# Two pairs of products of 64 stationary columns each made one product of 128, in a gated delta-rule layer followed by a GELU MLP

## Chip, cores, metric

One core of a Trainium2 chip. The metric is the device time of one execution in microseconds; several executions of each kernel on the same chip are compared. An execution counts as slow when its time is over 1.5% above the fastest of the same kernel; otherwise it is fast, and only fast ones are compared; a kernel that ran only once has no known state. The inputs are fp32, except for the two weight matrices of the MLP: these arrive as 64-bit words (a piece of 128 x 512 is 512 KB in the DMA list), and VectorE and ScalarE decode them to fp32 in the first part of the kernel. All products are fp32.

## The reference

```python
# deltanet: per batch and head, a 48 x 48 state, over 768 steps
k_n = k / (norm(k) + 1e-6)
for t in range(S):                       # B, H, S, D = 4, 8, 768, 48
    y[t]  = q[t] @ state
    v_old = state.T @ k_n[t]
    state = state + beta[t] * outer(k_n[t], v[t] - v_old)
# then, on y laid out as (3072, 384):
h = x @ w_in                             # 384 -> 2048
g = 0.5 * h * (1 + erf(h / sqrt(2)))
out = g @ w_out                          # 2048 -> 384
```

The kernel works in 12 chunks of 64 steps. A chunk is two units (`a` = 0, 1), each with 2 batches x 8 heads. With K, Q, V the chunk's rows and S the state, a unit needs K S and Q S, a triangular solve that gives U, then P^T U (P the masked products of K with Q) for its output and K^T U for the next state. These are small: contraction 48 or 64, 48 moving columns. (A product loads one operand, `lhsT`, into TensorE's array and streams the other, `rhs`, through it; they are called stationary and moving, and the trace lists the load as LDWEIGHTS on "PEld" and the streaming as MATMUL on "PE".) Between them TensorE does the MLP of the previous chunk: psH (first layer) and psO (second), with 128 x 128 stationary tiles. Other names in the timelines: psU is the solve, psG the products of K with K and Q, psJ joins the halves of the elimination that prepares the solve, and psT, psX and psB are transposes.

## The kernel before

A product of 64 x 64 uses a quarter of the 128 x 128 array, and the loops go round the four quarters. The part that a product uses is called its tile, rows x columns; a tile change below is a switch between products of different tile shape. In `QUADS` the first number is the half of the rows, the second that of the columns (in `next_state` the other way round). Every product is fp32 and shows as two instructions in the trace (two MATMUL, two LDWEIGHTS), so 16 products are 32 instructions.

```python
QUADS = [(0, 0), (1, 1), (0, 1), (1, 0)]
SIDES = [(0, 0), (1, 0), (0, 1), (1, 1)]

def state_product(u, x, psum):                      # x = 0: K S,  x = 1: Q S
    for j in range(NP):
        for r, p in QUADS:
            rows = slice(r * C, r * C + D)
            nc.tensor.matmul(psum(p, j, r), lhsT=u.KQt[rows, j, p, x, :],     # 64 columns
                             rhs=St[rows, u.a, p, j, :], start=True, stop=True)

def against_state(u):
    # ... (chunk 0 cut)
    state_product(u, 0, lambda p, j, r: psK[HALF[p], r, j, :])
    nc.vector.tensor_tensor(heads(u.W), psK, heads(u.V), op=ALU.subtract)
    nc.vector.tensor_tensor(u.W, u.W, gm..., op=ALU.mult)

def query(u):
    state_product(u, 1, lambda p, j, r: psQ[HALF[p ^ (j % 2)], j // 2, j % 2, r, :])
    for r in range(2):
        nc.scalar.copy(heads(u.y)[:, r], psQ[...])

def read(u):                                         # P^T U
    for k in range(NP // 2):
        for r in range(2):
            for p, s in SIDES:
                h = 4 * k + 2 * s + r
                nc.tensor.matmul(psY[HALF[p ^ s], p, h, :], lhsT=u.P[HALF[p], h, :],
                                 rhs=u.U[HALF[p], h, :], start=True, stop=True)
    # ... four additions of 64 x 192: x = psY + y

def next_state(u):                                   # K^T U
    for j in range(NP):
        for r, p in QUADS:
            nc.tensor.matmul(psS[HALF[r], p, j, :], lhsT=u.Kp[HALF[p], 2 * j + r, :],
                             rhs=u.U[HALF[p], 2 * j + r, :], start=True, stop=True)
    nc.vector.tensor_tensor(St[:, u.a], St[:, u.a], psS, op=ALU.add)

def state_steps(c):
    us = [tiles[c, a] for a in range(NA)]
    steps = [(1.0, fn, u) for fn in (against_state, query, solve, next_state, read) for u in us]
    return steps + [(0.5, turn, u) for u in us]
```

## Time and profile before

| | before |
|---|---|
| time, median | 755.5 us (754.5 to 755.7, 4 runs) |
| span of the profiled run | 753.3 us |
| TensorE busy, 170 us to the end | 577.2 of 583.3 us |
| VectorE busy, 60 to 170 us | 104.4 of 110 us |
| granted TensorE clock (share of full speed), whole span | 0.99 |

The table splits the span because two engines take turns in setting it: VectorE up to about 170 us, TensorE after that. The prediction shows the lines that say so. "Burst" below means one run of small products between full-size ones, and its price is the time from its start to the next burst's start, less what the full-size products between them stream for.

### The profile page before, as it was taken

How to read it: one execution, taken by the hardware profiler on the slowest of the kernel's cores; microseconds unless marked ns; L12 is line 12 of the kernel's file. 1: busy time of each engine (PE TensorE's matmuls, PEld its weight loads, DVE VectorE, ACT ScalarE, POOL GpSimd, SP SyncE). 2: the span in 40 equal slices, each digit the busy share in tenths (PEclk: the TensorE clock that was granted, in tenths of full speed). 3: DMA queues.
4: the chain of work that ended last, by engine and by line, in shares of the span. 5: the costliest groups of instructions: out<-in, count | busy, mean ns of one | idle time of the engine just before them, and what ended most of it. 6: DMA issues, size and time to landing. Idle time of an engine off the chain costs nothing.

```text
span 753.3 us, 19282 instructions
## 1 busy us (share of the span) xinstructions
PE 704.0 (93%) x8532; PEld 508.5 (68%) x8532; DVE 376.4 (50%) x855; ACT 249.4 (33%) x602; POOL 84.7 (11%) x91
## 2 busy tenths in 40 slices
PE   6549786899999999999999999999999999999997
PEld 5347553576687687687587687687687687586774
DVE  6988999996329722329822329822329821210100
ACT  3335633422553134352134352133352132122120
POOL 5051001203110002110012010012020010000000
PEclk9999999998999999999999999999999999999999
DMA  9807544400311101211101211001001000000000
GB/s 150 199 25 206 131 125 129 103 1 19 60 33 23 32 13 32 44 32 23 34 13 32 44 32 23 12 12 23 12 12 23 12 12 2 11 12 1 22 1 21
DMA packets 84515, 32.90 MB, mean 44 GB/s; under 512 B 77328, under 2 KB 80400, under 8 KB 84432
## 3 DMA queue, kind: packets, MB, share of 16 engines
q1 hardware_dynamic: 78384, 26.36, 16.0%
q10 hardware_dynamic: 5952, 5.12, 3.0%
q8 instruction: 67, 1.10, 0.6%
q0 software_dynamic: 96, 0.20, 0.1%
q14 instruction: 16, 0.13, 0.1%
HBM read 26.94 MB, written 4.72 MB: 42 GB/s over the span
## 4 chain that ended last, share of the span: by engine, by line
PE 77%; DVE 19%; issue 2%; DMA 1%; POOL 1%; ACT 0%; ACTq 0%; POOLq 0%; DVEq 0%
PE psO L544 30%; PE psH L535 30%; DVE tmp L359 3%; DVE Nu L361 3%; PE psT L283 2%; PE psG L293 2%; DVE w_e L204 2%; PE psU L470 2%; PE psJ L404 2%; PE psS L509 2%; PE psQ L447 2%; PE psK L447 2%; PE psJ L407 2%; PE psY L493 1%; DVE w_e L194 1%
## 5 line engine op out<-in xcount | busy, mean ns | idle before, releaser
L544 PE MATMUL psO<-w_out_sb,g 128*128 128x384 f32 x768 | 272.9, 500 | 10.2 <-DVE w_out_sb L205 10.2
L535 PE MATMUL psH<-xT,w_in_sb 128*128 128x256 f32 x1152 | 274.9, 388 | 3.4 <-DVE w_in_sb L205 3.0
L535 PEld LDWEIGHTS psH<-xT,w_in_sb 128*128 128x128 f32 x1152 | 213.1, 191 | 37.4 <-DVE w_in_sb L205 3.5
L544 PEld LDWEIGHTS psO<-w_out_sb,g 128*128 128x128 f32 x768 | 140.4, 192 | 97.2 <-DVE w_out_sb L205 15.6
L538 ACT ACTIVATE g<-psH 128x256 f32<-128x256 f32 x192 | 73.5, 383 | 177.4 <-PE psH L535 177.1
L361 DVE TENSOR_TENSOR Nu<-Nu,tmp 128x30 f32<-128x30 f32 (+9 forms) x180 | 61.9, 344 | 6.2
L359 DVE TENSOR_TENSOR tmp<-Nu 128x30 f32<-128x30 f32 (+9 forms) x180 | 61.8, 343 | 5.6
L253 POOL TENSOR_TENSOR n<-n,half 128x16 f32<-128x16 f32 x10 | 29.5, 2947 | 222.6 <-DVE n L242 222.6
L501 DVE TENSOR_TENSOR x<-psY,y 64x192 f32<-64x192 f32 x88 | 31.0, 353 | 42.3 <-PE psY L493 41.4
L307 DVE TENSOR_TENSOR P<-psG,mask 128x512 f32<-128x512 f32 x20 | 13.7, 690 | 72.8 <-ACT G L301 72.7
L512 DVE TENSOR_TENSOR St<-St,psS 128x384 f32<-128x384 f32 x22 | 12.2, 553 | 75.4 <-PE psS L509 75.0
L459 DVE TENSOR_TENSOR W<-psK,V 128x384 f32<-128x384 f32 x22 | 12.2, 555 | 73.6 <-PE psK L447 56.8
L475 ACT COPY U<-psU 64x192 f32<-64x192 f32 x92 | 28.8, 313 | 46.8 <-PE psU L470 46.0
L548 ACT COPY o_sb<-psO 128x384 f32<-128x384 f32 x24 | 11.5, 479 | 89.3 <-PE psO L544 89.3
L293 PE MATMUL psG<-KQt 48*64 48x128 f32 (+1 forms) x896 | 30.4, 286 | 3.9 <-ACT KQt L284 2.7
L522 ACT COPY xT<-psX 128x384 f32<-128x384 f32 x24 | 11.4, 477 | 68.0 <-PE psX L521 67.9
L293 PEld LDWEIGHTS psG<-KQt 48*64 48x64 f32 x896 | 24.9, 157 | 10.6 <-issue 4.8
L284 ACT COPY KQt<-psT 128x512 f32<-128x512 f32 x48 | 26.5, 589 | 9.1 <-PE psT L283 8.6
L383 POOL MEMSET Zf<- 32x512 f32 x23 | 12.2, 529 | 147.5 <-DVE Zf L374 145.5
L404 PE MATMUL psJ<-XM,G 32*32 32x32 f32 x768 | 15.5, 198 | 13.6 <-DVE XM L370 13.6
L415 DVE TENSOR_TENSOR XM<-psJ,gm 32x512 f32<-32x512 f32 (+1 forms) x26 | 16.9, 649 | 20.4 <-PE psJ L404 20.1
L196 ACT ACTIVATE w_e<-w_e,lim 128x384 uint32<-128x384 uint32 (+2 forms) x31 | 19.4, 625 | 23.0 <-DVE w_e L194 22.8
(100 smaller groups left out, 584.9 us busy)
## 6 DMA issues: line engine op xcount, KB each, us to landing
Qp<-in_q_dram SPq DMA_DIRECT2D x48, 96.0 KB, 3.4
V<-in_v_dram SPq DMA_DIRECT2D x48, 96.0 KB, 2.9
w_out_sb<-in_moe_w_in_dram SPq DMA_DIRECT2D x9, 512.0 KB, 5.3
out_dram<-o_sb ACTq DMA_DIRECT2D x48, 96.0 KB, 2.2
Zf<-in_moe_w_out_dram SPq DMA_DIRECT2D x8, 384.0 KB, 3.5
w_raw<-in_moe_w_out_dram SPq DMA_DIRECT2D x8, 384.0 KB, 3.1
Kp<-in_k_dram SPq DMA_DIRECT2D x28, 96.0 KB, 3.1
w_out_sb<-in_moe_w_in_dram SPq DMA_DIRECT2D x6, 256.0 KB, 4.4
```

Source lines behind the costliest of these rows:

```text
L253: nc.gpsimd.tensor_tensor(flat, flat, half, op=ALU.pow)
L284: nc.scalar.copy(u.KQt[:, :, :, x, :], psT.rearrange("q j (p n) -> q j p n", p=2))
L293: nc.tensor.matmul(psG[HALF[p], r, j, cols], lhsT=u.KQt[rows, j, p, 0, :], rhs=u.KQt[rows, j, p].rearrange("q x n -> q (x n)")[:, cols], s ...
L359: nc.vector.tensor_tensor(tmp, nu[:, j + 1:, j:j + 1].to_broadcast([128, n, j]), nu[:, j:j + 1, 0:j].to_broadcast([128, n, j]), op=ALU.mult)
L361: nc.vector.tensor_tensor(nu[:, j + 1:, 0:j], nu[:, j + 1:, 0:j], tmp, op=ALU.add)
L404: nc.tensor.matmul(psJ[low_, 0, col], lhsT=raw[top, u, HB:C], rhs=xm[top, u, :], start=True, stop=True)
L447: nc.tensor.matmul(psum(p, j, r), lhsT=u.KQt[rows, j, p, x, :], rhs=St[rows, u.a, p, j, :], start=True, stop=True)
L475: copies[i % len(copies)](pairs(u.U[HALF[p]], s), pairs(psU[HALF[p ^ s], p], s))
L501: nc.vector.tensor_tensor(dst, src, pairs(u.y[HALF[p ^ s]], s), op=ALU.add)
L535: nc.tensor.matmul(psH, lhsT=w_in_sb[:, m, f * 128:(f + 1) * 128], rhs=xTs[c][:, m, :], start=(m == 0), stop=(m == NM - 1))
L538: nc.scalar.activation(gs[f], psH, ACT.Gelu)
L544: nc.tensor.matmul(u.psO, lhsT=gs[f][:, u.a * 128:(u.a + 1) * 128], rhs=w_out_sb[:, f, :], start=(f == 0), stop=(f == NF - 1))
```

## The change

K^T and Q^T of a unit already lie beside each other in SBUF, so one product with 128 stationary columns gives K S in the lower 64 output partitions and Q S in the upper 64. For K^T U with P^T U the same is reached by putting P next to K, for which K is loaded from DRAM a second time.

```diff
-    NKS, NQS, NKW = 6, 4, 10
+    NKS, NQS = 4, 4
+    KP = [cpool.tile([128, H, 2, C], F32, name=f"KP{i}") for i in range(4)]
 ...
+    def place(c):
+        for a in range(NA):
+            u = tiles[c, a]
+            u.KP = KP[u.n % 4 if u.n < 8 else (u.n - 4) % len(KP)]
+            u.P = u.KP[:, :, 1, :]
+            fetch_in(u.KP[:, :, 0, 0:D], k, u)
 ...                                        # against_state
+        for p in range(2):
+            for j in range(NP):
+                for r in range(2):
+                    rows = slice(r * C, r * C + D)
+                    nc.tensor.matmul(psK[:, r, p, j, :],
+                                     lhsT=u.KQt[rows, j, p].rearrange("q x n -> q (x n)"),
+                                     rhs=St[rows, u.a, p, j, :], start=True, stop=True)
+        for p in range(2):
+            nc.vector.tensor_tensor(heads(u.W[HALF[p]]), psK[HALF[0], :, p], heads(u.V[HALF[p]]),
+                                    op=ALU.subtract)
         nc.vector.tensor_tensor(u.W, u.W, gm..., op=ALU.mult)
+        u.y = wk.tile([128, H, D], F32, tag="y", name="y")
+        for p in range(2):
+            nc.scalar.copy(heads(u.y[HALF[p]]), psK[HALF[1], :, p])
 ...
+    def use(u):
+        for h in range(H):
+            for p in range(2):
+                nc.tensor.matmul(u.psY[:, p, h, :],
+                                 lhsT=u.KP[HALF[p], h].rearrange("q x n -> q (x n)"),
+                                 rhs=u.U[HALF[p], h, :], start=True, stop=True)
 ...                                        # next_state: two additions of 64 x 384 from psY
 ...                                        # read: two additions of 64 x 384 from psY
-        steps = [(1.0, fn, u) for fn in (against_state, query, solve, next_state, read) for u in us]
+        steps = [(1.0, fn, u) for fn in (against_state, solve, outputs) for u in us]
```

Cut: the loads' places in the plan, the hand-ordered first chunk, the memsets of the padding.

More of the change, by code (lines that the diff above doesn't have):

```diff
@@ L86 @@
     tiles = {}
-    K_late = []
     def fetch_in(dst, src, u, queues=(nc.sync, nc.sync)):
@@ L100 @@
             u.Qp = Qp[u.n % NQS]
-            if u.n < NKW:
-                u.Kp = Kp[u.n % NKS]
+            u.Kp = Kp[u.n % NKS]
     def load(c):
@@ L108, in load @@
             u = tiles[c, a]
-            if u.n >= NKW:
-                u.Kp = K_late[(u.n - NKW) % len(K_late)]
             fetch_in(u.Kp[:, :, 0:D], k, u)
             fetch_in(u.Qp[:, :, 0:D], q, u)
+    def place(c):
+        if c >= NC:
+            return
+        for a in range(NA):
[3 more added lines that the diff above has]
+            fetch_in(u.KP[:, :, 0, 0:D], k, u)
     def load_v(c):
@@ L135 @@
         nc.gpsimd.memset(Kp[i][:, :, D:], 0.0)
+        nc.gpsimd.memset(KP[i][:, :, 0, D:], 0.0)
     for p in range(2):
@@ L302, in products @@
         if 1 in part:
-            u.P = wk.tile([128, H, C], F32, tag="P", name="P", bufs=6)
             if u.c < 2:
@@ L440 @@
     SIDES = [(0, 0), (1, 0), (0, 1), (1, 1)]
-    def state_product(u, x, psum):
-        for j in range(NP):
-            for r, p in QUADS:
-                rows = slice(r * C, r * C + D)
-                nc.tensor.matmul(psum(p, j, r), lhsT=u.KQt[rows, j, p, x, :],
-                                 rhs=St[rows, u.a, p, j, :], start=True, stop=True)
     def against_state(u):
@@ L452, in against_state @@
         gm = gms[u.c // 2][:, u.t]
+        u.y = None
         if u.c == 0:
@@ L456, in against_state, with solve @@
             return
-        psK = dn("psK")[:, :, 0:NP * D].rearrange("q r (j d) -> q r j d", d=D)
-        state_product(u, 0, lambda p, j, r: psK[HALF[p], r, j, :])
-        nc.vector.tensor_tensor(heads(u.W), psK, heads(u.V), op=ALU.subtract)
+        psK = dn("psK")[:, :, 0:2 * NP * D].rearrange("q r (p j d) -> q r p j d", p=2, d=D)
+        for p in range(2):
[8 more added lines that the diff above has]
+                                    op=ALU.subtract)
         nc.vector.tensor_tensor(u.W, u.W, gm.unsqueeze(2).to_broadcast([128, H, D]),
                                 op=ALU.mult)
-    def solve(u, copies=(nc.scalar.copy,)):
+        u.y = wk.tile([128, H, D], F32, tag="y", name="y")
+        for p in range(2):
+            nc.scalar.copy(heads(u.y[HALF[p]]), psK[HALF[1], :, p])
+    def solve(u, copy=nc.scalar.copy):
         zf = Zf[(u.c // 2) % 2]
@@ L473, in solve, with read @@
         u.U = wk.tile([128, H, D], F32, tag="U", name="U")
-        for i, (p, s) in enumerate(SIDES):
-            copies[i % len(copies)](pairs(u.U[HALF[p]], s), pairs(psU[HALF[p ^ s], p], s))
-    def query(u):
-        u.y = None
-        if u.c == 0:
-            return
-        psQ = dn("psQ")[:, :, 0:NP * D].rearrange("q r (k s d) -> q k s r d", s=2, d=D)
-        state_product(u, 1, lambda p, j, r: psQ[HALF[p ^ (j % 2)], j // 2, j % 2, r, :])
-        u.y = wk.tile([128, H, D], F32, tag="y", name="y")
-        for r in range(2):
-            nc.scalar.copy(heads(u.y)[:, r], psQ[:, :, :, r, :].rearrange("q k s d -> q (k s) d"))
-    def read(u, copies=(nc.scalar.copy,)):
-        psY = dn("psY")[:, :, 0:DM].rearrange("q p (h d) -> q p h d", d=D)
-        for k in range(NP // 2):
-            for r in range(2):
-                for p, s in SIDES:
-                    h = 4 * k + 2 * s + r
-                    nc.tensor.matmul(psY[HALF[p ^ s], p, h, :], lhsT=u.P[HALF[p], h, :],
-                                     rhs=u.U[HALF[p], h, :], start=True, stop=True)
+        for p, s in SIDES:
+            copy(pairs(u.U[HALF[p]], s), pairs(psU[HALF[p ^ s], p], s))
+    def use(u):
+        u.psY = dn("psY")[:, :, 0:DM].rearrange("q p (h d) -> q p h d", d=D)
+        for h in range(H):
[3 more added lines that the diff above has]
+                                 rhs=u.U[HALF[p], h, :], start=True, stop=True)
+    def read(u, copy=nc.scalar.copy):
         u.x = wk.tile([128, H, D], F32, tag="x", name="x")
-        for i, (p, s) in enumerate(SIDES):
-            dst, src = pairs(u.x[HALF[p]], s), pairs(psY[HALF[p ^ s], p], s)
+        for p in range(2):
             if u.y is None:
-                copies[i % len(copies)](dst, src)
+                copy(u.x[HALF[p]], u.psY[HALF[1], p])
             else:
-                nc.vector.tensor_tensor(dst, src, pairs(u.y[HALF[p ^ s]], s), op=ALU.add)
+                nc.vector.tensor_tensor(u.x[HALF[p]], u.psY[HALF[1], p], u.y[HALF[p]], op=ALU.add)
     def next_state(u):
@@ L505, in next_state, with outputs @@
             return
-        psS = dn("psS")[:, :, 0:NP * D].rearrange("q p (j d) -> q p j d", d=D)
-        for j in range(NP):
-            for r, p in QUADS:
-                nc.tensor.matmul(psS[HALF[r], p, j, :],
-                                 lhsT=u.Kp[HALF[p], 2 * j + r, :], rhs=u.U[HALF[p], 2 * j + r, :],
-                                 start=True, stop=True)
-        nc.vector.tensor_tensor(St[:, u.a], St[:, u.a], psS, op=ALU.add)
+        for r in range(2):
+            part = u.psY[HALF[0]].rearrange("q p (j r) d -> q p r j d", r=2)[:, :, r]
+            nc.vector.tensor_tensor(St[HALF[r], u.a], St[HALF[r], u.a], part, op=ALU.add)
+    def outputs(u):
+        use(u)
+        next_state(u)
+        read(u)
     def turn(u):
@@ L587 @@
         fetch(n)
+    for c in range(2):
+        place(c)
     new_group(0)
@@ L620 @@
         against_state(u)
-        query(u)
     for u in first:
@@ L631 @@
         scale_v(u)
-    on = [(nc.scalar.copy,), (nc.vector.tensor_copy,)]
+    on = [nc.scalar.copy, nc.vector.tensor_copy]
     decode(0)
@@ L637 @@
     signed(0)
+    use(first[0])
     read(first[0], on[0])
@@ L640 @@
     signed(1)
+    use(first[1])
     read(first[1], on[1])
@@ L653, in late @@
         more = ctx.enter_context(tc.tile_pool(name="late", bufs=1))
-        for i in range(4):
-            K_late.append(more.tile([128, H, C], F32, name=f"Kl{i}"))
-            nc.gpsimd.memset(K_late[i][:, :, D:], 0.0)
-        K_late.extend(Kp)
+        for i in range(4, 6):
+            KP.append(more.tile([128, H, 2, C], F32, name=f"KP{i}"))
+            nc.gpsimd.memset(KP[i][:, :, 0, D:], 0.0)
     plan = [at(c + 1, c + 2, ffn_steps(c)) for c in range(NC)]
+    plan += [at(t, t + 0.001, [(1.0, place, c)])
+             for c, t in [(2, 1.05), (3, 1.605), (4, 2.64)]]
+    plan += [at(c - 2.02 + 0.45 * (c % 2 == 0), c - 2.01 + 0.45 * (c % 2 == 0), [(1.0, place, c)]) for c in range(5, NC)]
     plan += [at(0.985, 1.26, decode_steps(NM, n_in)), at(1.26, 1.65, decode_steps(n_in, NW)), at(1.66, 1.67, [(1.0, late)])]
```

## The prediction

> **What bounds the kernel now.** I read the page first (shares, the 40 slices, the chain that ended last), then the windows view to split the span, then the timeline of TensorE alone to price one burst of small products, then the groups by form for the other engines.
>
> ```profile
> PE 704.0 (93%) x8532; PEld 508.5 (68%) x8532; DVE 376.4 (50%) x855; ACT 249.4 (33%) x602; POOL 84.7 (11%) x91
> PE   6549786899999999999999999999999999999997
> DVE  6988999996329722329822329822329821210100
> DMA  9807544400311101211101211001001000000000
> PE 77%; DVE 19%; issue 2%; DMA 1%; POOL 1%; ACT 0%; ACTq 0%; POOLq 0%; DVEq 0%
> ```
>
> TensorE is full from slice 9 on, VectorE before that. The chain has 77% of TensorE and 19% of VectorE, and next to no DMA. The windows view makes the border exact:
>
> ```profile
> 170.00:753.30 583.30, 577.21 (x6772) 414.90 (x6772) 224.54 (x493) 180.50 (x452) 54.76 (x48) 0.99 0.11 22
> 60.00:170.00 110.00, 93.62 (x886) 65.90 (x878) 104.41 (x240) 47.98 (x106) 10.43 (x9) 0.97 0.44 112
> ```
>
> Columns: stretch, length, then busy time of PE, PEld, DVE, ACT, POOL. From 170 us TensorE works 577 of 583 us, so a microsecond of TensorE occupancy removed there is a microsecond of span. From 60 to 170 us VectorE works 104 of 110 us (decoding weights, the second elimination): there VectorE's instructions count and TensorE's do not.
>
> How long does TensorE hold still for one burst of small products? Busy sums cannot say it (matmuls overlap: 704 records of psK at 226 ns would be 159 us, the row says 15.4). Starts in the timeline can:
>
> ```profile
> 442.90 1.10 PE L293 MATMUL psG<-KQt 48*64 48x128 f32 x32
> 443.93 2.86 PE L535 MATMUL psH<-xT,w_in_sb 128*128 128x256 f32 x12
> 446.72 1.10 PE L293 MATMUL psG<-KQt 48*64 48x128 f32 x32
> ...
> 451.83 0.68 PE L447 MATMUL psK<-St,KQt 48*64 48x48 f32 x32
> 452.45 2.86 PE L535 MATMUL psH<-xT,w_in_sb 128*128 128x256 f32 x12
> 455.23 0.68 PE L447 MATMUL psK<-St,KQt 48*64 48x48 f32 x32
> ```
>
> From one psK to the next is 3.40 us. The 12 psH in it take 12 x 215.8 ns = 2.59 us (the chain view has runs of 96 psH in 20.72 us). So a burst of 32 costs 0.81 us. The same for psG: 446.72 - 442.90 - 2.59 = 1.23 us. A psH pass streams 256 columns in 215.8 ns and psO 384 in 322.5 (64 in 20.65 us): 0.84 ns per moving column. psG streams 128 columns, 107.5 ns, on four 64x64 tiles at once: 26.9 ns each, 0.86 us for 32, which leaves 0.37 us. psK streams 48, which would be 40 ns on four tiles, 10 ns each, 0.32 us; with the same 0.37 to 0.38 us left over it has 0.43 us, 13.3 ns each. So I read a burst as 0.38 us of going into and out of the small tiles, plus 32 x 13.3 ns set by something other than streaming. The early, half-speed part tells what:
>
> ```profile
> 10.29 1.49 PE L575 MATMUL psB<-ident,w_in_sb 32*128 32x32 f32 x12
> 11.71 1.11 PE L283 MATMUL psT<-ident,Kp 128*128 128x128 f32 x4
> ...
> 58.17 1.96 PE L509 MATMUL psS<-U,Kp 64*64 64x48 f32 x64
> 60.06 2.86 PE L535 MATMUL psH<-xT,w_in_sb 128*128 128x256 f32 x6
> ```
>
> psB loads 128 stationary columns for only 32 moving ones, always in the same rows: 1.42 us / 12 = 118 ns, where streaming needs 54 at half speed. psS: 1.89 us / 64 = 29.5 ns, or 26.6 without one change of tiles. psD (32 stationary columns, 64 of them in 0.83 us) takes 13 ns each at the same speed. The cost follows the **stationary columns**: about 0.83 ns per column at half speed, 0.42 at full, with two loads at a time where the rows alternate between upper and lower half: 64 x 0.42 / 2 = 13.3. No floor per instruction explains 26.6 beside 13.
>
> **What the Trainium skill says.** TensorE: Matmul & The Clock Gate, section LDWEIGHTS, says that a load costs by its columns and not by the contraction length, columns / 1.2 ns; the early psB (118 ns for 128) is near it, the full-speed psK shows half of it. Its Part 1 tells of a clock at half rate until the engine has been busy; the trace agrees in durations (four psT start to start 1.0 us at the beginning, 0.43 us at 437 us), though the granted-clock column reads 0.97 to 1.00 throughout. Its Part 3 lets a load overlap running matmuls when the row group differs; two loads side by side is what psK's 13.3 ns asks for, and all bursts of before alternate halves, as both new loops do. TensorEngine Tiling (Array Packing), Key Properties, says that changing the tiling mode drains the engine: that is the 0.38 us per burst here (0.19 us per change). Whether 64x128 tiles change as dearly, no run of before shows.
>
> **The change part by part.**
>
> (1) K S and Q S: 32 + 32 instructions of 64 stationary columns become 32 of 128. The loads are 32 x 13.3 x 2 = 0.85 us before and 32 x 26.7 = 0.85 us after; streaming on two tiles instead of four is 20 ns each and stays hidden under 26.7. Nothing is gained in the array; what goes is one burst's two tile changes. (2) K^T U with P^T U: the same, except in the last chunk, where there was no state update and the read alone now loads 128 columns: 0.43 us more for each of 2 units.
>
> (3) The sum on the path. I laid the TensorE order of both kernels beside each other from the second elimination's first joining product on and priced each row as above (psH 431.6 ns and psO 645 for their two passes, transposes 108.5, psG 53.4, the 64-column products and psJ 26.7, the new ones 53.4, 190 ns per change of tile shape). Before comes to 571 us; measured are about 578 from 170.7 us to the end of TensorE's work, so the pricing holds to 1.2%. Tile changes fall from 244 to 184: -60 x 0.19 = -11.4 us. (Two bursts saved by each of 18 units and one by each of 2 would be 76 changes; some bursts already share a change with a neighbour, and some new ones meet a 64x64 burst.) The last chunk adds +0.85. Ten transposes are issued before that point in the new order, where TensorE has time: -1.1. Sum **-11.6 us**.
>
> (4) VectorE. Its time goes by the free size, not the partitions:
>
> ```profile
> L501 DVE TENSOR_TENSOR x<-psY,y 64x192 f32<-64x192 f32 x88 | 31.0, 353 | 42.3 <-PE psY L493 41.4
> L512 DVE TENSOR_TENSOR St<-St,psS 128x384 f32<-128x384 f32 x22 | 12.2, 553 | 75.4 <-PE psS L509 75.0
> L459 DVE TENSOR_TENSOR W<-psK,V 128x384 f32<-128x384 f32 x22 | 12.2, 555 | 73.6 <-PE psK L447 56.8
> ```
>
> W: one instruction of 555 becomes two on 64 partitions with the same 384 elements, +0.55. The state: likewise two, +0.55. x: four of 353 become two of about 553, -0.3. So +0.8 us per unit. Only four units lie before 170 us: +0.8 for each of chunk 1, and in chunk 0 +0.55 each, with 0.35 off one unit's copies, while 1.4 us of waiting for a separate psS (at 59.3 and 60.2 us) goes. Together about **+1.3 us**. After 170 us VectorE is under half busy and it costs nothing.
>
> (5) The second load of K: 48 more transfers of 96 KB, each about 3.1 us to landing. In the new order they wait for TensorE's use of the old tile alone, and the masking into the same tile does not wait for them. The eight early ones stand behind the first six weight pieces and delay loads not needed for another 25 us. After slice 9 DMA is at one to two tenths. I count 0. (6) ScalarE: y is two copies of 384 instead of 192 elements (479 for 322 ns), +0.3 us per unit, hidden.
>
> Total: 755.7 - 11.6 + 1.3 = 745.4, called **745 us** (-1.4%).
>
> **The rivals.** (A) Streaming or something faster, not loading, sets the pace on 64x128 tiles: 20 ns each gives -20.2 us on TensorE, 735 us. For: the two halves are only inferred to load together, and a load might go faster without column tiles. Against: psB and psK agree on one rate. (B) Loads of 128 columns do not run side by side (in before, neighbours always differed in columns too): 53.3 ns each, +22.4 us, 780 us. For: no run shows two 128-column loads at once. Against: alternate rows, and the Skill's Part 3. (C) A wait takes the gain: each product's PSUM tile is held for two reads more, from a pool of two, and the weight fetches stand behind K's second load in one queue. It would give back 2 to 8 us, 747 to 753 us. Against: three steps per unit instead of five are spread over the same stretch, so latency has more room.
>
> **Range and chances.** The load-bound case carries about two thirds and lies at 742 to 749 with small waits; A about a fifth, B a twentieth, C the rest. Range 734 to 755. Faster by over 2% means below 740.6: 0.27. Slower by over 2%: 0.04. Within 2%: 0.69.
>
> **What would show it.** Right: in the steady stretch the new psK and psY bursts of 32 take about 1.23 us between full-size runs, TensorE is still 99% busy after 170 us, the gain per two chunks (113.5 us before) is about 2.5 us. A burst near 1.02 us is A, near 2.1 is B, new idle time ahead of psU, psK or psG on TensorE is C. The start of the second elimination's joins (170.7 us) should come about 1 us later; several us later would mean that fetches were held up. Wrong altogether if changing to 64x128 tiles costs nothing, or more than 0.38 us a burst.

## The result

The changed kernel takes **787.0 us** (785.1 to 787.7, 4 runs) against 755.5: 1.042 times the time, 95% interval 1.039 to 1.044. A ratio here and below is the mean time of one kernel's fast runs over that of the other's fast runs of the same rounds, so not quite the ratio of the medians. It is slower by 4%, where I had said 1.4% faster and had given this outcome 4 chances in 100.

Page of the changed kernel: busy times, TensorE's slices, the chain that ended last; then the windows view from 170 us on.

```profile
PE 738.0 (94%) x7124; PEld 549.0 (70%) x7124; DVE 392.5 (50%) x853; ACT 258.1 (33%) x600; POOL 84.3 (11%) x91
PE   6468897989999999999999999999999999999997
PE psO L548 30%; PE psH L539 29%; PE psY L494 6%; PE psK L463 5%; DVE Nu L368 3%; DVE tmp L366 3%; PE psT L291 2%; PE psG L301 2%; PE psJ L411 2%; PE psJ L414 2%; PE psU L482 2%; DVE w_e L212 1%; DMA Kp<-in_k_dram 1%; DVE w_out_sb L213 1%; DVE w_out_sb L207 1%
```

```profile
170.00:783.30 613.30, 604.94 (x5552) 447.47 (x5550) 242.06 (x503) 187.48 (x450) 54.62 (x48) 0.99 0.13 25
```

TensorE is as full as before and has fewer instructions (7,124 for 8,532), yet is busy longer; psY and psK are now 11% of the chain, where psS, psQ, psK and psY together were 7%. So it is mainly the new bursts themselves that are long. TensorE's timeline in the steady stretch shows them (columns: start, length, engine, line, operation, names, shapes, count):

```profile
469.30 1.99 PE L463 MATMUL psK<-St,KQt 48*128 48x48 f32 x32
471.22 4.34 PE L539 MATMUL psH<-xT,w_in_sb 128*128 128x256 f32 x18
475.48 1.99 PE L463 MATMUL psK<-St,KQt 48*128 48x48 f32 x32
...
491.02 1.99 PE L494 MATMUL psY<-U,KP 64*128 64x48 f32 x32
492.94 5.43 PE L548 MATMUL psO<-w_out_sb,g 128*128 128x384 f32 x16
498.30 1.99 PE L494 MATMUL psY<-U,KP 64*128 64x48 f32 x32
```

From one psY to the next are 7.28 us, of which 16 psO stream for 5.16: a wide burst costs **2.12 us**, where two narrow ones cost 1.62 and I had said 1.23. From one psK to the next are 6.18 us with 3.88 of psH: 2.30 us, so 0.18 more than psY. That is a second, smaller loss, and the waits of the two kernels show it. First the changed kernel, then the one before (columns: engine, line, what it waited for, us in total, times, longest):

```profile
ACT y L473 <- DVE W L467: 56.4, 22, 3.1
PEld psH L539 <- ACT g L542: 6.7, 20, 0.8
DVE x L502 <- PE psY L494: 3.5, 1, 3.5
```

```profile
ACT y L485 <- PE psQ L447: 5.6, 19, 0.7
PEld psH L535 <- ACT g L538: 1.1, 3, 0.5
```

ScalarE's copy of y used to wait for its product. Now it reads the tile that VectorE subtracts from, is ordered behind that subtraction, and ScalarE stands; the GELU g behind it comes late, and the weight load of a psH waits for the buffer that g frees: 20 times, once for each psK burst after 170 us.

**Where the 30.1 us went** (783.4 less 753.3, the spans of the two profiled runs). The second elimination's first joining product, psJ, starts at 175.3 us instead of 170.7: +4.6 us in the part that VectorE sets. TensorE's timeline, before and then changed:

```profile
170.70 2.79 PE L404 MATMUL psJ<-XM,G 32*32 32x32 f32 x128 [1.86 <-DVE XM L370]
```

```profile
175.29 3.62 PE L411 MATMUL psJ<-XM,G 32*32 32x32 f32 x128 [3.59 <-DVE XM L377]
```

The rest takes 608.1 us instead of 582.6: +25.5. In it are 20 merged K S / Q S bursts at +0.50 us (2.12 - 1.62), 18 merged K^T U / P^T U at +0.50, two reads of the last chunk at +1.31 (2.12 - 0.81): 21.6; the stall behind g, 20 x 0.18 = 3.6; the ten transposes moved ahead, -1.1. Together 24.1, so 1.4 us of this part stay unaccounted for. Of these, 0.8 are in the joining products shown above, 3.62 us for 2.79; it does not come from wide products, for b2_again, which has none, shows 3.62 as well.

The early 4.6 us: in the half-speed beginning the two first psY bursts took 7.0 us (2.2 for psY and 1.9 for psS before), and VectorE waited 3.5 us for them (the third line of the changed kernel's waits above):

```profile
51.84 7.07 PE L494 MATMUL psY<-U,KP 64*128 64x48 f32 x64 [0.61 <-ACT U L487]
```

The waits for a separate psS went, 1.4 us, and other waits were 0.3 us shorter. VectorE's instructions fill 155.3 us up to the first psJ instead of 152.5 (windows view), so the added ones are 2.8 us, for which I had reckoned 2.7: 3.5 - 1.4 - 0.3 + 2.8 = 4.6.

### The profile page after: what moved, and what is told of

Read it like the earlier page. It is cut to its first block, busy times and chain, and to the rows that moved or that the text cites. A ratio compares the mean times of both kernels' runs of the same rounds, so it can differ in the third digit from the quotient of the medians.

```text
span 783.4 us, 16543 instructions
## 1 busy us (share of the span) xinstructions
PE 738.0 (94%) x7124; PEld 549.0 (70%) x7124; DVE 392.5 (50%) x853; ACT 258.1 (33%) x600; POOL 84.3 (11%) x91
## 4 chain that ended last, share of the span: by engine, by line
PE 80%; DVE 15%; ACT 1%; issue 1%; DMA 1%; POOL 1%; ACTq 0%; SPq 0%; POOLq 0%; DVEq 0%
PE psO L548 30%; PE psH L539 29%; PE psY L494 6%; PE psK L463 5%; DVE Nu L368 3%; DVE tmp L366 3%; PE psT L291 2%; PE psG L301 2%; PE psJ L411 2%; PE psJ L414 2%; PE psU L482 2%; DVE w_e L212 1%; DMA Kp<-in_k_dram 1%; DVE w_out_sb L213 1%; DVE w_out_sb L207 1%
## 5 line engine op out<-in xcount | busy, mean ns | idle before, releaser
L548 PE MATMUL psO<-w_out_sb,g 128*128 128x384 f32 x768 | 269.2, 498 | 3.8 <-DVE w_out_sb L213 3.7
L467 DVE TENSOR_TENSOR W<-psK,V 64x384 f32<-64x384 f32 x44 | 24.2, 550 | 107.4 <-PE psK L463 85.6
L511 DVE TENSOR_TENSOR St<-St,psY 64x384 f32<-64x384 f32 x44 | 24.1, 547 | 76.8 <-PE psY L494 76.5
L494 PEld LDWEIGHTS psY<-U,KP 64*128 64x128 f32 x768 | 48.3, 199 | 13.6 <-issue 12.3
L494 PE MATMUL psY<-U,KP 64*128 64x48 f32 x768 | 51.4, 286 | 1.2 <-ACT U L487 0.6
L314 DVE TENSOR_TENSOR KP<-psG,mask 128x512 f32<-128x512 f32 x20 | 13.7, 691 | 70.0 <-ACT G L309 69.9
L463 PEld LDWEIGHTS psK<-St,KQt 48*128 48x128 f32 x704 | 41.3, 188 | 8.1 <-issue 4.2
L463 PE MATMUL psK<-St,KQt 48*128 48x48 f32 x704 | 44.2, 274 | 0.0
L473 ACT COPY y<-psK 64x384 f32<-64x384 f32 x44 | 20.9, 475 | 56.8 <-DVE W L467 56.4
L504 DVE TENSOR_TENSOR x<-psY,y 64x384 f32<-64x384 f32 x44 | 24.6, 560 | 21.1 <-PE psY L494 20.0
```

The source lines that it names most:

```text
L463: nc.tensor.matmul(psK[:, r, p, j, :], lhsT=u.KQt[rows, j, p].rearrange("q x n -> q (x n)"), rhs=St[rows, u.a, p, j, :], start=True, stop= ...
L467: nc.vector.tensor_tensor(heads(u.W[HALF[p]]), psK[HALF[0], :, p], heads(u.V[HALF[p]]), op=ALU.subtract)
L494: nc.tensor.matmul(u.psY[:, p, h, :], lhsT=u.KP[HALF[p], h].rearrange("q x n -> q (x n)"), rhs=u.U[HALF[p], h, :], start=True, stop=True)
L504: nc.vector.tensor_tensor(u.x[HALF[p]], u.psY[HALF[1], p], u.y[HALF[p]], op=ALU.add)
L548: nc.tensor.matmul(u.psO, lhsT=gs[f][:, u.a * 128:(u.a + 1) * 128], rhs=w_out_sb[:, f, :], start=(f == 0), stop=(f == NF - 1))
```

## The experiments

All kernels gave the right result. The kernel before was run again on the same chips: medians 755.6 us (first four kernels) and 755.1 (second four).

### a1_narrow: split each wide product again, keep all else

```diff
-                for r in range(2):
+                for r, x in QUADS:
-                    nc.tensor.matmul(psK[:, r, p, j, :],
-                                     lhsT=u.KQt[rows, j, p].rearrange("q x n -> q (x n)"),
+                    nc.tensor.matmul(psK[HALF[x], r, p, j, :],
+                                     lhsT=u.KQt[rows, j, p, x, :],
...                                        # the same in use(), with QUADS over (p, x)
```

> The changed kernel with each product of 128 stationary columns split into two of 64 with alternating halves of rows and columns; PSUM layout, vector work, transfers and order of everything else stay. Theory 1 (loads of 128 columns do not run side by side, so the wide bursts cost 1.73 us instead of 0.85): psK and psY bursts of 64 instructions take about 0.85 + 0.38 us, and the time falls by about 33 us against the changed kernel, to 745 to 758. Theory 2 (the loss is new waits: second load of K, longer-held PSUM, more vector work): the time stays within 5 us of the changed kernel's 787.

Measured: 749.9 us, ratio to the kernel before 0.993 (0.991 to 0.994), 37 us under the changed kernel. A burst, in TensorE's timeline:

```profile
469.62 1.15 PE L494 MATMUL psY<-U,KP 64*64 64x48 f32 x64
470.70 5.43 PE L548 MATMUL psO<-w_out_sb,g 128*128 128x384 f32 x16
476.05 1.15 PE L494 MATMUL psY<-U,KP 64*64 64x48 f32 x64
```

6.43 - 5.16 = 1.27 us for twice the instructions. The second load of K, the PSUM layout and the vector work are those of the changed kernel, so the width of the stationary operand (and with it the number of tiles, two instead of four) is the cause, and theory 2 falls as the main one.

### a2_stream: is it the load, and do the two halves of the rows work side by side?

```diff
+                    n = 2 * D if i < 2 * NP - 1 else D
-                    nc.tensor.matmul(psK[:, r, p, j, :],
+                    nc.tensor.matmul(flatK[:, r, i * D:i * D + n],      # overwritten by the next product
-                                     rhs=St[rows, u.a, p, j, :], start=True, stop=True)
+                                     rhs=flatS[rows, i * D:i * D + n], start=True, stop=True)
...                                        # use()
-        for h in range(H):
-            for p in range(2):
+        for p in range(2):
+            for h in range(H):
```

> The changed kernel with two edits that keep the result: psK streams 96 columns instead of 48 (the second half is overwritten by the next product), and psY runs through all heads on the upper row half, then all on the lower, instead of alternating. If the load of 128 columns is what takes 54 ns each and streams of the two halves run side by side (80/2 = 40 ns), psK bursts keep their 1.92 us start to start. If the streams do not run side by side, 80 ns each, 2.75 us. If load and stream of one instruction follow each other (13 + 40), about 94 ns each, 3.2 us. psY in order of halves: if loads are one after the other whatever the rows, the burst keeps 1.92 us; if alternating halves bought something, it is longer.

Measured: 843 us (one run, state unknown, so only the bursts are read), TensorE's timeline:

```profile
444.59 1.99 PE L467 MATMUL psK<-St,KQt 48*128 48x96 f32 x32
446.51 4.32 PE L543 MATMUL psH<-xT,w_in_sb 128*128 128x256 f32 x18
...
461.78 3.36 PE L498 MATMUL psY<-U,KP 64*128 64x48 f32 x32
465.07 4.54 PE L552 MATMUL psO<-w_out_sb,g 128*128 128x384 f32 x8
```

psK with twice the moving columns keeps its 1.92 us: streaming is hidden, the load of the stationary columns is the pace. psY in order of halves takes 3.29 us instead of 1.92: the two halves do work side by side when they alternate. That contradicts the reason of my rival B, though its number came true.

### b1_orders: which tiles load at the same time?

```diff
-        for j in range(NP):
-            for r, p in QUADS:
+        if x == 0:      # psK: neighbours in different row halves, one column half
+            order = [(j, r, p) for p in range(2) for j in range(NP) for r in range(2)]
+        else:           # psQ: neighbours in different column halves, one row half
+            order = [(j, r, c ^ (j % 2)) for r in range(2) for j in range(NP) for c in range(2)]
+        for j, r, p in order:
...                                        # next_state: runs of eight instructions in one tile
-        for j in range(NP):
-            for r, p in QUADS:
+        for r, p in QUADS:
+            for j in range(NP):
```

> The kernel before with only the order of its small products changed, same result. psK: neighbours alternate row halves within one column half. psQ: neighbours alternate column halves within one row half. psS: runs of eight in one tile. psU and psY unchanged as controls (0.61 us start to start). Theory 1a (two loads run together only where their column halves differ, so a 128-column load can never have a partner): psK 26.7 ns each, 1.03 us to the next product; psQ stays 0.61; psS 1.03. Theory 1b (two loads run together where the row halves differ, as I predicted with; a 128-column load is slow for some other reason): psK stays 0.61, psQ 1.03, psS 1.03. If both must differ, both are 1.03. If loads never pair and each 64-column load is 13 ns, all stay 0.61, but then streaming may show in psS (40 ns each, 1.5 us).

Measured: 785 us (one run, state unknown, so only the bursts are read), TensorE's timeline; starts of the bursts and of what follows them:

```profile
470.04 0.95 PE L450 MATMUL psK<-St,KQt 48*64 48x48 f32 x32
470.92 2.86 PE L538 MATMUL psH<-xT,w_in_sb 128*128 128x256 f32 x12
...
477.37 0.95 PE L450 MATMUL psQ<-St,KQt 48*64 48x48 f32 x32
478.25 2.86 PE L538 MATMUL psH<-xT,w_in_sb 128*128 128x256 f32 x12
...
492.77 1.48 PE L512 MATMUL psS<-U,Kp 64*64 64x48 f32 x32
494.18 2.85 PE L547 MATMUL psO<-w_out_sb,g 128*128 128x384 f32 x8
```

psK and psQ take the same, 0.88 us instead of 0.61; psS takes 1.41; the controls psU and psY keep 0.61. None of the theories said so. It matters little whether neighbours differ in rows or in columns; what counts is **how many different tiles** take turns: four, two, one. A look at single starts, with windows that end ever later, gives the price of one tile. The number is how many have started. First the MATMULs of psK of the kernel before, in windows to 451.86, 451.95 and 452.01 us:

```profile
451.83 0.27 PE L447 MATMUL psK<-St,KQt 48*64 48x48 f32 x4
451.83 0.33 PE L447 MATMUL psK<-St,KQt 48*64 48x48 f32 x8
451.83 0.39 PE L447 MATMUL psK<-St,KQt 48*64 48x48 f32 x12
```

then the weight loads of psK of the changed kernel, to 469.31, 469.42 and 469.53 us:

```profile
469.30 0.19 PEld L463 LDWEIGHTS psK<-St,KQt 48*128 48x128 f32 x2 [0.33 <-DVE Nu L359]
469.30 0.30 PEld L463 LDWEIGHTS psK<-St,KQt 48*128 48x128 f32 x4 [0.33 <-DVE Nu L359]
469.30 0.41 PEld L463 LDWEIGHTS psK<-St,KQt 48*128 48x128 f32 x6 [0.33 <-DVE Nu L359]
```

The narrow ones come in fours, one for each tile, all four within 0.02 us, and the next four some 0.058 us later (the single records of the trace; the lines merge them). The wide ones come in twos, and the next two 0.11 us later. So one tile takes **58 ns for 64 stationary columns and 112 ns for 128** (0.9 ns per column), and all tiles load at once. 8 x 58 = 0.46 us for a narrow burst of 32, 16 x 112 = 1.79 us for a wide one; what is left of 0.81 and 2.12 for changing tiles is then nearly the same, 0.35 and 0.33 us. A tile that works alone keeps these times: 0.058 us from load to load in b1's psS, 0.112 in a2's psY (single records). Where two runs meet, the next tile begins before the last is done: in b1's psS its first load comes 0.27 us after the first of the run before, which needs 8 x 58 = 0.46. That is why these bursts are shorter than a plain sum: 1.41 us to the next product, not 32 x 58 ns + 0.35 = 2.21, for psS, 0.88, not 1.28, for psK and psQ, and 3.29, not 3.91, for a2's psY.

### a4_half: only K^T U / P^T U narrow again

The edit is the second half of a1's.

> The changed kernel with the narrow form for psY only; K S with Q S stays one product of 128 columns. If the cost is in the bursts and adds up by them: 18 psY bursts get 2.12 - 1.27 = 0.85 us shorter and the last two as well, 17 us, plus some 2 us in the half-speed beginning (7.0 us for two bursts there, 3.5 when narrow): 768. If the two wide products share one cost that is paid once (for instance a wait further down that either causes), it is near 787 or near 750 instead.

Measured: 767.6 us (765.2 to 771.4), ratio 1.018 (1.014 to 1.021). From the first psJ to the end the profiled run takes 591.1 us (765.9 less 174.8) instead of 608.1: 17.0 less, which is 20 x 0.85. The cost adds up by bursts, as reckoned.

### a3_yfirst: the copy of y ahead of the subtraction

```diff
+        u.y = wk.tile([128, H, D], F32, tag="y", name="y")
+        for p in range(2):
+            nc.scalar.copy(heads(u.y[HALF[p]]), psK[HALF[1], :, p])
         for p in range(2):
             nc.vector.tensor_tensor(heads(u.W[HALF[p]]), psK[HALF[0], :, p], ...)
...                                        # and taken away behind it
```

> The changed kernel with the two copies of y issued ahead of the subtraction that reads the same PSUM tile, so that ScalarE waits for TensorE alone and VectorE waits for ScalarE instead. In the changed kernel weight loads of psH wait 6.7 us in all for the GELU that stands behind those copies (1.1 us before), and TensorE shows about 0.19 us lost behind each of 20 psK bursts. Theory 1 (that stall is a second, smaller cost, apart from the 128-column loads): the run of 18 psH after a psK burst falls from 4.26 to about 4.08 us and the time falls by 3 to 4 us, to 783 to 784. If the stall is only moved, to the wait of the subtraction or to psU, the time stays at 787.

Measured: 782.4 us (781.8 to 784.4), ratio 1.037 (1.035 to 1.039) where the changed kernel had 1.042. The two ran on different occasions, each against the kernel before; their intervals (up to 1.0386, and from 1.0394) do not overlap, but the 4.6 us between the medians is a rough size. In both kernels the runs with the lower granted clock are the longer ones: at 0.991 the changed kernel took 785.1 us and this one 781.8 to 782.9, at 0.984 they took 787.7 and 784.4. At the same clock the gain is about 3 us. In the profiled runs the stretch from the first psJ to the end fell from 608.1 us to 604.5 (782.7 less 178.2), so by 3.6, which is 20 x 0.18, as theory 1 had it. Waits and TensorE's timeline of this kernel:

```profile
PEld psH L539 <- ACT g L542: 1.5, 1, 1.5
```

```profile
470.53 1.99 PE L463 MATMUL psK<-St,KQt 48*128 48x48 f32 x32
472.45 4.15 PE L539 MATMUL psH<-xT,w_in_sb 128*128 128x256 f32 x18
476.53 1.99 PE L463 MATMUL psK<-St,KQt 48*128 48x48 f32 x32
```

The 18 psH take 4.08 us again instead of 4.26, and the burst with them 2.12, the same as psY.

### b2_joined and b2_again: keep the narrow products, join the bursts

```diff
-        psK = dn("psK")[:, :, 0:NP * D]...
+        u.psKQ = dn("psKQ")
+        psK = u.psKQ[:, :, 0:NP * D]...
         state_product(u, 0, ...)
+        query(u)                          # Q S right behind K S, into u.psKQ[:, :, NP * D:2 * NP * D]
...
-        steps = [(1.0, fn, u) for fn in (against_state, query, solve, next_state, read) for u in us]
+        steps = [(1.0, fn, u) for fn in (against_state, solve, outputs) for u in us]   # outputs: next_state, read
```

> The kernel before with its narrow products, but K S and Q S of a unit issued as one burst into one PSUM tile, and state update and read as neighbours: the tile changes that the change wanted to save, without 128-column loads, second load of K or more vector work. By the pricing of the prediction TensorE saves 61 changes x 0.19 = 11.6 us after the second elimination starts: 741 to 747 us. If changes of tile shape cost nothing and the leftover 0.38 us is per instruction group, 755.

Measured: 742.9 us in four fast runs, ratio 0.983 (0.982 to 0.985). Its profiled run, 1009 us at a granted clock of 0.674, is not used.

> The same kernel as b2_joined, whose profile fell into a state with the clock at two thirds; again for a profile in the fast state. 742 to 743.5 us; bursts of 64 narrow products take about 0.93 + 0.34 us between full-size runs, the second elimination's joins begin within 1 us of the kernel before (170.7), and weight loads of psH wait under 2 us for GELU.

Measured: 743.2 us, ratio 0.985 (0.983 to 0.987). TensorE's timeline:

```profile
447.50 1.15 PE L447 MATMUL psKQ<-St,KQt 48*64 48x48 f32 x64
448.58 4.15 PE L539 MATMUL psH<-xT,w_in_sb 128*128 128x256 f32 x18
452.66 1.15 PE L447 MATMUL psKQ<-St,KQt 48*64 48x48 f32 x64
```

5.16 - 3.88 = 1.28 us for both products, one pair of tile changes less than the 1.62 of two bursts. The joins begin at 170.55 us and psH waits 0.9 us in all for GELU. From there to the end are 571.4 us (741.9 less 170.55) where the kernel before takes 582.6: 11.2 less, and the pricing had 11.6. This is the gain that the change was after, 12 us, without the wide products. Against a1_narrow, which has the same bursts, it is 6.7 us faster: a1 still has the stall behind g (3.6 us) and the dearer beginning (its joins begin at 173.5 us, 3.0 later, with VectorE at work for 155.8 us up to there instead of 152.5).

### b3_pairs: one step further

The edit is shown against b2_joined; `both` calls `fn` for each of the two units.

```diff
-        steps = [(1.0, fn, u) for fn in (against_state, solve, outputs) for u in us]
+        steps = [(2.0, both, fn, us) for fn in (against_state, solve)] + [(1.0, outputs, u) for u in us]
```

> b2_joined with one more step of the same kind: the K S / Q S bursts of a chunk's two units issued back to back, and their solves too. Over the order of instructions the changes of tile shape fall from 183 to 145 against b2_joined. At 0.17 to 0.19 us each that is 6.5 to 7.2 us: 735.5 to 737, which would be over 2% under the kernel before. If both accumulation tiles being taken at once makes the following products wait, it stays at 740 to 743.

Measured: **737.1 us** (736.2 to 737.7), ratio 0.977 (0.975 to 0.978): over 2% faster than the kernel before, and the best of all. 38 tile changes fewer than b2 gave 6.1 us, 0.16 us each; b2's 61 fewer than before gave 12 us, 0.20 each. From the first psJ on, the profiled runs say 0.19 and 0.18 (7.3 us of b3 against b2_again, 11.2 of b2_again against before).

## Why the prediction was wrong, point by point

- **Failed: "32 x 13.3 x 2 = 0.85 us before and 32 x 26.7 = 0.85 us after"**, with the reading behind it, "about 0.83 ns per column at half speed, 0.42 at full, with two loads at a time". Runs showed 0.9 ns per column at full speed and as many loads at a time as there are tiles. The 13.3 ns of before was not half of 27 but a quarter of 53 to 58. A wide tile holds two narrow ones: each load takes twice as long *and* only half as many run together. Half as many instructions at four times the price each: 1.79 us where 0.93 was. Less the saved tile changes, this makes 21.6 of the 30.1 us on the 40 wide bursts after 170 us, and it is also behind the 3.5 us at the beginning.
- **How I came to it.** I fitted one rate to the half-speed psB, 118 ns for 128 columns. psB is a transpose, and psK is not. At the same half speed the wide psY of the changed kernel took 7.0 us for 64 in twos, 213 ns from one two to the next (single records). That the transpose makes the difference is my reading; no run isolates it. The Trainium skill's page TensorE: Matmul & The Clock Gate says in its Terms that LDWEIGHTS and MATMUL have a transpose mode that is faster for fp32; I did not look there. Its section LDWEIGHTS gives columns / 1.2 ns: 53 and 107. I set that aside as half too large, and it was right within 10%: the measurement shows 58 and 112. A second look at the trace would have shown the fours. That my pricing of the kernel before came out within 1.2% (571 of 578 us) was no test: its 13.3 ns had been taken from the same bursts, and half of 27 and a quarter of 53 give the same sum.
- **Rival B was right in size, wrong in reason.** It said 53.3 ns each, +22.4 us on TensorE, 2.1 us a burst and 780 us; measured were +21.9 (the 25.5 from the joins on, less the stall's 3.6), 2.12 and 787. But "do not run side by side" is false (a2: 3.29 us in order of halves, 1.92 alternating). I gave it a twentieth because I took the parallel loading as an argument against it.
- **Held: the tile changes.** 0.19 us per change, 11.4 us for 60: b2 without wide products gained 12 us, b3 6.1 for 38. The counting over the instruction orders told both times beforehand: 741 to 747 for b2 (742.9), 735.5 to 737 for b3 (737.1).
- **Held: who bounds what.** TensorE 98.6% busy after 170 us; the second load of K made no wait on the path that the traces show (a1, which has it, differs from b2 by the two costs named above). The chain of the changed kernel does name Kp transfers; a late one lands at 89.9 us, but VectorE was at work until then and had no gap before its next instruction. (DMA after slice 9 reads nought to three tenths, not "one to two".)
- **Rival C came true in part,** and by another wait than those I named: not PSUM buffers or the fetch queue, but the copy of y ordered behind VectorE's subtraction on the same tile, 3.6 us. My part (6), "hidden", counted the copy's length and not what it waits for.
- **Mis-sized: the beginning,** +1.3 predicted, +4.6 measured. The wide load at half clock put 3.5 us of waiting on VectorE, which follows from the same failed step. VectorE's own part was right (2.7 reckoned, 2.8 measured; halves of 64 partitions took 550 and 547 ns, as I had assumed), but the items listed, 2.7 - 0.35 - 1.4, make 0.95 and not 1.3. My sign "several us later would mean that fetches were held up" would have misled: the joins came 4.6 us later for other reasons.

## What to carry to other kernels

Before merging small products, count the tiles that load at once: where loads and not streaming set the pace, as here with 48 moving columns, two products of 64 columns on four tiles cost less than one of 128 on two, because the load time goes with the columns and the parallelism with the tiles. What small bursts lose to full-size neighbours is the change of tile shape, and that is saved by issuing narrow bursts back to back. When two consumers on different engines come to read one PSUM tile, look which is ordered behind which, and put first the one whose engine has the critical work queued behind it.

## What the Trainium skill lacked or had wrong

- TensorE: Matmul & The Clock Gate, section LDWEIGHTS: right (53 and 107 ns by its formula; 58 and 112 measured per tile at full clock). It gives one figure for both clock rates and for transposes: here 128 columns took 213 ns for the product psY at half speed, and 118 for the transpose psB at the same speed.
- The same page, Part 3: loads overlap matmuls in flight "only when row_grp differs". Here two tiles in one row half with different column halves went as fast as two in different row halves: 0.88 us for psQ and for psK in b1_orders.
- TensorEngine Tiling (Array Packing), Key Properties: says that a mode change drains, without a price. Here 0.16 to 0.20 us a change (61 fewer gave 12 us, 38 fewer 6.1 us), for 64x128 tiles about as for 64x64 (0.33 and 0.35 us left over in a burst).
- The same page, When to Use Tiling: gives the tiling factor by the small dimension. It sets no cost of 64x128 tiles beside one of 64x64 when the load sets the pace: 2.12 us against 1.27 for the same products here.
